# The last block's outputs finished bank by bank, with product P7 in two PSUM banks

## The chip, the cores and the metric

The kernel runs on one core of one Trainium2 chip. The metric is the device time of one execution in microseconds (us); a smaller number is better. A profile covers one such execution. Its span, from the first to the last instruction of the program, is a little shorter than the time of that execution.

## The reference, cut to what matters

A depthwise causal convolution with softmaxed taps (one set of 7 taps per head) is followed by two matrix products with a SiLU between them. All is fp32.

```python
w = softmax(weight, axis=-1)                       # (8 heads, 7 taps)
out[b, s, head, :] = sum_k w[head, k] * x_pad[b, s + k, head, :]
x = out.reshape(32768, 192)
h = x @ w_in                                       # (32768, 2048)
g = h * (1.0 / (1.0 + np.exp(-h)))                 # silu(h)
return g @ w_out                                   # (32768, 192)
```

## The kernel before, in words

The 32,768 tokens are worked in 32 blocks of 1,024, each of two token tiles of 512 (`TB`). The feature axis lies on the partitions, so a token tile is 512 columns of a PSUM bank. For each block VectorE computes the convolution, TensorE the products of `x @ w_in` (L442), ScalarE copies and applies SiLU (L457, L463), VectorE adds (L466), and TensorE then computes `g @ w_out` (L513). Work of the next block's convolution is interleaved into the present block by the strings of `PLAN`; `pin` keeps every engine's instructions in the order in which the program issues them.

From the second block on, both matrix products are done with seven instead of eight block products (Winograd's form of Strassen's algorithm). For `g @ w_out` the 2x2 split is: two token tiles against two halves of the 192 output channels, 96 (`HD`) each. The 2,048 hidden features are summed in four steps j = 0 to 3 (`NJ`), each with two sub-steps e. For each j VectorE first forms four combinations of silu(h) with `sum_g` (L483), named `t.j0` to `t.j3`: 128x1024 subtractions. They lie in tiles of the pool `tpool` (tag "t", three buffers), two combinations to a tile.

`out_slot(b, j, i, e)` issues the matmuls of one output bank i. A bank has 128 partitions and a product only 96 rows, so partitions 0 to 95 hold one product and partitions 96 to 127 a third of another: bank 0 is P1 with a third of P2, bank 1 is P3 with a third of P2, bank 2 is P6 with the last third of P2, bank 3 is P7 with a third of P4, bank 4 is P5 with a third of P4, and bank 5 holds the last third of P4 as four pieces of 128 columns. Each 32-row quarter is a matmul of its own; the profile shows two hardware matmuls for each. Banks 0 and 1 and P2 use silu(h) itself; bank 2 needs `t.j1`, bank 3 `t.j2` and `t.j3`, bank 4 `t.j0` and `t.j3`, bank 5 `t.j3`.

The outputs `c[0]` to `c[3]` (96 x 512 rows of the tile `cmb`, channel half i // 2 of token tile i % 2) are then sums of products: c0 = P1 + P2, c1 = P1 + P6 + P3 + P5, c2 = P1 + P6 + P7 + P4, c3 = P1 + P6 + P7 + P5. ScalarE copies the thirds of P2 into a tile `y` and those of P4 into a tile `x_`, so that they stand on the right partitions for VectorE. Each c[i] is transposed by VectorE into `osb` and stored by three DMAs, two issued from the queue of SP and one from that of ScalarE (L685).

In all blocks but the last these sums run beside the next block's matmuls. For the last block the program runs j = 0 and 1 through `down` with the plan's remaining slots (which include `t.20`), and then calls `finish` (L654), where the change lies. There TensorE's order before is: for j = 2, then j = 3, banks 2, 4, 3, 5; then bank 0 for both j; then bank 1 for both j, in two halves of 256 columns. VectorE forms each j's combinations ahead of that j's matmuls. The sums begin when banks 2 to 5 are full: c1 = P6 (L691), c2 and c3 with P7 and P5, P4 added to c2; then, when bank 0 is full, P1 to c3, c2 and c1, with c3 and c2 stored whole; ScalarE's copies of P1 and a third of P2 (L717, L718) follow. Last come, for each half, P3 to c1 (VectorE), the copy of the last third of P2 (L722), the store of c1, P2 to c0 (GpSimd, L724) and the store of c0. The adds, transposes and copies through `vec` and `act` are recorded under L111.

Of the kernel before, what the change touches and what calls it, by code (L numbers as in the profile page):

```python
# [9 lines left out]
F32 = mybir.dt.float32  # L10
I32 = mybir.dt.int32
AF = mybir.ActivationFunctionType
ALU = mybir.AluOpType
# [4 lines left out]
def kernel(  # L18
# [24 lines left out]
    nc = tc.nc  # L43
# [6 lines left out]
    P = 128  # L50
# [4 lines left out]
    TB = 512  # L55
    TT = 2 * TB
    NB = NT // TT
    NCH = DFF // P
    NM = NCH // 2
    NJ = NM // 2  # L60
    SQ = 32
    HD = D // 2
    NP = HD // SQ
# [6 lines left out]
    xpool = ctx.enter_context(tc.tile_pool(name="xp", bufs=1))  # L70
    tpool = ctx.enter_context(tc.tile_pool(name="tp", bufs=3))
# [31 lines left out]
    def pin(ins):  # L103
        return tc.keep_in_program_order(ins)
# [8 lines left out]
    vec, act = Pinned(nc.vector), Pinned(nc.scalar)  # L113

    def bank():
        return psum.tile([P, TB], F32, tag="ps", name="ps")
# [171 lines left out]
    for e in range(2):  # L288
        half = hot[R * e : R * e + R]
# [24 lines left out]
    for k in range(NK):  # L314
# [4 lines left out]
            op=ALU.mult,  # L319
# [98 lines left out]
    bk, us, sums, cmbs, accs = {}, {}, {}, {}, {}  # L418
# [32 lines left out]
    def sums_h(b, name, m):  # L451


        if name[0] == "s":
            u = us[b, m, name[1]] = upool.tile([P, TB], F32, tag="u", name="u")
            copy = nc.vector.tensor_copy if name == "s2" else nc.scalar.copy
            pin(copy(u, bk[b, m, "1"]))  # L457
            return
        g = g_of(b, m, int(name[1]) - 1, int(name[2]) - 1)
        if name == "C21":  # L460
            pin(nc.scalar.activation(g, bk[b, m, "1"], AF.Silu))
        elif name[0] == "g":
            pin(nc.scalar.activation(g, g, AF.Silu))  # L463
        else:
            i, bn = {"C11": ("1", "b"), "C22": ("3", "d"), "C12": ("2", "d")}[name]
            pin(nc.vector.tensor_tensor(g, us.pop((b, m, i)), bk[b, m, bn], op=ALU.add))  # L466
# [18 lines left out]
    def out_slot(b, j, i, e, half=None):  # L485

        g = [gs[b, j, a] for a in range(2)]
        w, x_ = wo[j], wx[j]  # L490
        if i not in accs.setdefault(b, {}):
            accs[b][i] = bank()

        def t(k):
            return sums[b, j][k // 2][:, k % 2, :].rearrange("p (e t) -> p e t", e=2)

        a_ = [[w[:, a, :, HD * u : HD * u + HD] for a in range(2)] for u in range(2)]
        forms = {
            1: lambda: (a_[0][0], g[0][:, 0]),
            2: lambda: (a_[0][1], g[1][:, 0]),  # L500
            3: lambda: (x_[:, 2], g[1][:, 1]),
            4: lambda: (a_[1][1], t(3)),
            5: lambda: (x_[:, 0], t(0)),
            6: lambda: (x_[:, 1], t(1)),
            7: lambda: (a_[1][0], t(2)),
        }
        own, other, c = ((1, 2, 0), (3, 2, 1), (6, 2, 2), (7, 4, 0), (5, 4, 1), (4, 4, 2))[i]
        for q in range(4):
            lhs, rhs = forms[own if q < NP else other]()
            k = c if i == 5 or q == NP else q  # L510
            to = slice(0, TB // 4) if i == 5 else slice(0, TB) if half is None else ts(half, TB // 2)
            pin(
                nc.tensor.matmul(  # L513
                    accs[b][i][SQ * q : SQ * q + SQ, to],
                    lhs[:, e, SQ * k : SQ * k + SQ],
                    rhs[:, e, ts(q, TB // 4) if i == 5 else to],
                    start=j == 0 and e == 0,
                    stop=j == NJ - 1 and e == 1,
                    skip_group_check=True,
                )  # L520
            )

    def down(b, j):

        for i in (0, 1, 2, 4, 3, 5) if j < NJ - 1 else (0, 1, 2, 3, 5, 4):
            for e in range(2):
                out_slot(b, j, i, e)
                yield
        for a in range(2):
            del gs[b, j, a]  # L530
# [63 lines left out]
    osbs = {}  # L594
# [21 lines left out]
    def step(b, token):  # L616

        if token[0] == "-":
            b, token = b - 1, token[1:]
        name, arg = token.split(".") if "." in token else ("", "")  # L620
        if b < 0 or b >= NB or not name or (b, token) in did:
            return
        did.add((b, token))
        digits = [int(c) for c in arg]
        if name[0] in "PE":
            product(b, digits[0], name)
        elif name[0] in "sCg":
            if b:
                sums_h(b, name, digits[0])
        elif name == "t":  # L630
            sum_g(b, *digits)
        elif name[0] in "Mzyx":
            merge(b, name)
        elif name == "o":
            turn_out(b, *digits)
        elif b + 1 < NB:
            {"i": turn_in, "v": conv, "w": win}[name](b + 1, *digits)
            if name == "v" and digits[1] == K - 1 and (b, "down") in did:
                spread(b + 1, digits[0])
                if digits[0] == NK - 1 and b + 2 < NB:  # L640
                    load(b + 2)
# [12 lines left out]
    def finish(b):  # L654


        late = (NJ - 2, NJ - 1)
        for j in late:
            for k in (0, 1, 3, 2):
                step(b, f"t.{j}{k}")  # L660
            for i in (2, 4, 3, 5):
                for e in range(2):
                    out_slot(b, j, i, e)
        acc, n = accs[b], HD
        cmb = xpool.tile([P, 4, TB], F32, tag="cmb", name="cmb")
        cmbs[b] = [cmb]
        c = [cmb[0:n, i, :] for i in range(4)]
        y, x_ = (upool.tile([P, TB], F32, tag="u", name="u") for _ in range(2))

        def part(t, k):  # L670
            return t[SQ * k : SQ * k + SQ, :]

        def add(out_, u, v):
            vec.tensor_tensor(out_, u, v, op=ALU.add)

        def store(i, cols, rows_=slice(0, n)):

            if b not in osbs:
                osbs[b] = tpool.tile([P, 4, TB // SQ, SQ], F32, tag="t", name="osb")
            osb = osbs[b][:, i, :, :].rearrange("p k c -> p (k c)")  # L680
            vec.transpose(osb[rows_, cols], cmb[rows_, i, cols])
            ks = slice(cols.start // SQ, cols.stop // SQ)
            for q in range(rows_.start // SQ, rows_.stop // SQ):
                ch = HD * (i // 2) + SQ * q
                (nc.sync, nc.scalar, nc.sync)[q % 3].dma_start(  # L685
                    out=out_v[2 * b + i % 2][:, ks, ch : ch + SQ],
                    in_=osbs[b][SQ * q : SQ * q + SQ, i, ks, :],
                )

        every = slice(0, TB)  # L690
        pin(nc.scalar.copy(c[1], acc[2][0:n, :]))  # L691
        pin(nc.scalar.copy(part(y, 2), acc[2][n:P, :]))
        pin(nc.scalar.copy(part(x_, 1), acc[4][n:P, :]))
        add(c[2], c[1], acc[3][0:n, :])
        pin(nc.scalar.copy(part(x_, 0), acc[3][n:P, :]))
        add(c[3], c[2], acc[4][0:n, :])
        add(c[1], c[1], acc[4][0:n, :])
        for q in range(4):
            pin(
                nc.scalar.copy(  # L700
                    part(x_, 2)[:, ts(q, TB // 4)], acc[5][SQ * q : SQ * q + SQ, 0 : TB // 4]
                )
            )
        add(c[2], c[2], x_[0:n, :])
        for j in late:
            for e in range(2):
                out_slot(b, j, 0, e)
        for half in range(2):
            for j in late:
                for e in range(2):  # L710
                    out_slot(b, j, 1, e, half)
            if half == 0:
                for k in (3, 2):
                    add(c[k], c[k], acc[0][0:n, :])
                    store(k, every)
                add(c[1], c[1], acc[0][0:n, :])
                pin(nc.scalar.copy(c[0], acc[0][0:n, :]))  # L717
                pin(nc.scalar.copy(part(y, 0), acc[0][n:P, :]))  # L718
        for half in range(2):
            cols = slice(half * TB // 2, (half + 1) * TB // 2)  # L720
            add(c[1][:, cols], c[1][:, cols], acc[1][0:n, cols])
            pin(nc.scalar.copy(part(y, 1)[:, cols], acc[1][n:P, cols]))  # L722
            store(1, cols)
            nc.gpsimd.tensor_tensor(c[0][:, cols], c[0][:, cols], y[0:n, cols], op=ALU.add)  # L724
            store(0, cols)


    for k in range(NK):
# [41 lines left out]
    for b in range(1, NB):  # L770
# [9 lines left out]
        slots = (None for j in range(NJ // 2 if last else NJ) for _ in down(b, j))  # L780
        for s, _ in zip(plan[NU:], slots):
            run(b, [s])
        assert next(slots, 0) == 0
    finish(NB - 1)


# [28 lines left out]
```

## Time and profile before

| | |
|---|---|
| Time, median of 4 runs | 2420.8 us (2420.28 to 2420.85) |
| The profiled execution's own time | 2420.28 us |
| Its span | 2418.5 us |
| Mean granted TensorE clock | 0.998 |
| Busy: TensorE / VectorE / ScalarE / GpSimd | 2387.2 / 2073.9 / 991.0 / 69.7 us |
| Share of the chain that ended last: PE / DMA | 98% / 1% |
| Last block's L513 matmuls begin | 2373.5 us after the span's start |

A profile names engines PE (TensorE; PEld is its weight load), DVE (VectorE), ACT (ScalarE), POOL (GpSimd) and SP; a q behind the name is the engine's sequencer or DMA queue. The chain that ended last follows the work back from the last instruction, at each step to what released it. A row of the timeline has start, duration, engine, line, operation, output<-input, shapes and, in brackets, the idle time before it and what ended that. All but some 45 us of the span lie ahead of the stage that the change touches.

### The profile page before, as it was taken

The page shows a single profiled execution, that of the slowest core. Times are in us where ns is not written, and L with a number is a line of the kernel's source. Part 1 is how long each engine was busy: PE and PEld are TensorE (multiplying, and loading weights), DVE is VectorE, ACT ScalarE, POOL GpSimd, SP SyncE. Part 2 cuts the span into 40 slices and gives each one's busy share as a digit, 9 for nine tenths or more (in the row PEclk, how much of TensorE's full clock was granted, in tenths as well). Part 3 has the DMA queues.
Part 4 walks back from the last instruction along what each step waited for, and adds up shares of the span by engine and source line. Part 5 has one row for each costly group of instructions (what it writes and reads, how often), then busy time and mean ns, then how long its engine had stood idle before and what let it go on. Part 6 is the DMA issues. An engine that isn't in the chain of part 4 may idle for free.

```text
span 2418.5 us, 43131 instructions
## 1 busy us (share of the span) xinstructions
PE 2387.2 (99%) x17776; PEld 937.3 (39%) x17776; DVE 2073.9 (86%) x2821; ACT 991.0 (41%) x1857; POOL 69.7 (3%) x98
## 2 busy tenths in 40 slices
PE   6999999999999999999999999999999999999998
PEld 3334433334433344333343333443334433334433
DVE  8889888898888888888988889888889888898876
ACT  3234533345433345333454334543334533345432
POOL 3300000000000000000000000000000000000000
PEclk9999999999999999999999999999999999999999
DMA  8321222222222212222222222122222222222220
GB/s 157 75 44 39 38 44 53 44 44 38 36 53 51 42 32 43 46 53 40 40 40 40 53 47 46 33 36 53 53 41 40 36 45 53 43 43 39 36 40 14
DMA packets 454085, 111.65 MB, mean 46 GB/s; under 512 B 423936, under 2 KB 429056, under 8 KB 453888
## 3 DMA queue, kind: packets, MB, share of 16 engines
q1 hardware_dynamic: 450064, 106.89, 23.8%
q8 instruction: 139, 2.28, 0.4%
q0 software_dynamic: 480, 1.58, 0.3%
q10 hardware_dynamic: 3344, 0.42, 0.1%
q14 instruction: 58, 0.48, 0.1%
HBM read 31.49 MB, written 25.17 MB: 23 GB/s over the span
## 4 chain that ended last, share of the span: by engine, by line
PE 98%; DMA 1%; DVE 0%; ACT 0%; SPq 0%; issue 0%; POOLq 0%; POOL 0%; ACTq 0%
PE ps L442 49%; PE ps L513 46%; PE ps L541 2%; PE ps L406 1%; DMA dup<-nat 0%; SPq L127 0%; DMA tail<-xt 0%; DVE nat L356 0%; DMA wexp<-in_weight_dram 0%; DMA nat<-in_x_dram 0%; ACT g L111 0%; ACT two L111 0%; DVE cmb L111 0%; DVE osb L111 0%; DVE two L111 0%
## 5 line engine op out<-in xcount | busy, mean ns | idle before, releaser
L442 PE MATMUL ps<-dup,ws 64*128 64x512 f32 x2480 | 869.9, 589 | 0.0
L513 PE MATMUL ps<-g,wo 128*32 128x512 f32 x2984 | 662.2, 592 | 0.0
L466 DVE TENSOR_TENSOR g<-u,ps 128x512 f32<-128x512 f32 x744 | 486.1, 681 | 119.1 <-PE ps L442 89.8
L442 PE MATMUL ps<-win,wr 64*128 64x512 f32 x1488 | 567.7, 589 | 0.0
L513 PE MATMUL ps<-t,wo 128*32 128x512 f32 (+1 forms) x4464 | 500.7, 450 | 0.0
L463 ACT ACTIVATE g<-g 128x512 f32<-128x512 f32 x744 | 444.8, 631 | 97.3 <-DVE g L466 97.3
L442 PEld LDWEIGHTS ps<-dup,ws 64*128 64x128 f32 x2480 | 363.0, 187 | 292.0 <-issue 277.9
L513 PE MATMUL ps<-t,wx 128*32 128x512 f32 x2976 | 452.9, 592 | 0.0
L356 DVE SCALAR_TENSOR_TENSOR nat<-xt,taps,nat 128x512 f32<-128x512 f32 x576 | 432.2, 751 | 18.7 <-ACT nat L351 3.8
L442 PE MATMUL ps<-dup,wr 64*128 64x512 f32 x992 | 419.9, 596 | 0.0
L457 ACT COPY u<-ps 128x512 f32<-128x512 f32 x496 | 278.1, 589 | 228.7 <-PE ps L442 225.7
L580 ACT COPY cmb<-ps 96x512 f32<-96x512 f32 x30 | 17.5, 582 | 805.3 <-PE ps L513 805.3
L483 DVE TENSOR_TENSOR t<-g,t 128x1024 f32<-128x1024 f32 x248 | 303.5, 1224 | 18.7 <-PE ps L513 8.3
L483 DVE TENSOR_TENSOR t<-g 128x1024 f32<-128x1024 f32 x248 | 299.9, 1220 | 22.8 <-PE ps L513 22.8
L442 PEld LDWEIGHTS ps<-win,wr 64*128 64x128 f32 x1488 | 233.4, 187 | 175.6 <-issue 147.2
L513 PEld LDWEIGHTS ps<-t,wo 128*32 128x32 f32 x4464 | 178.3, 110 | 222.6 <-issue 204.6
L442 PE MATMUL ps<-win,ws 64*128 64x512 f32 x496 | 242.2, 589 | 0.0
L513 PE MATMUL ps<-g,wx 128*32 128x512 f32 (+1 forms) x1512 | 234.6, 585 | 0.0
L513 PEld LDWEIGHTS ps<-t,wx 128*32 128x32 f32 x2976 | 121.9, 110 | 277.6 <-issue 268.3
L592 DVE TENSOR_TENSOR cmb<-cmb,ps 96x512 f32<-96x512 f32 x150 | 102.3, 682 | 135.2 <-ACT u L577 133.1
L442 PEld LDWEIGHTS ps<-dup,wr 64*128 64x128 f32 x992 | 160.5, 187 | 128.2 <-issue 114.0
L513 PEld LDWEIGHTS ps<-g,wo 128*32 128x32 f32 x2984 | 169.4, 110 | 98.3 <-issue 98.3
(66 smaller groups left out, 1206.8 us busy)
## 6 DMA issues: line engine op xcount, KB each, us to landing
dup<-nat SPq DMA_DIRECT2D x384, 128.0 KB, 2.3
nat<-in_x_dram SPq DMA_DIRECT2D x382, 64.0 KB, 2.4
out_dram<-osb SPq DMA_DIRECT2D x376, 64.0 KB, 2.0
raw<-in_moe_w_in_dram SPq DMA_DIRECT2D x16, 192.0 KB, 5.3
raw<-in_moe_w_out_dram SPq DMA_DIRECT2D x8, 384.0 KB, 3.9
ws<-wr POOLq DMA_DIRECT2D x8, 192.0 KB, 3.2
xt<-xt SPq DMA_DIRECT2D x31, 4.5 KB, 1.9
tail<-xt SPq DMA_DIRECT2D x24, 4.5 KB, 1.9
```

The source lines that it names most:

```text
L356: nc.vector.scalar_tensor_tensor(out=dst, in0=src, scalar=tap, in1=dst, op0=ALU.mult, op1=ALU.add)
L406: nc.tensor.matmul(hs[a, n, e], rows(wr[j], e)[:, a, k, :], rows(d, e)[:, n, k, :], start=k == 0, stop=k == NK - 1,)
L442: nc.tensor.matmul(bk[b, m, bn], rows(w, half), rows(v, half), start=first, stop=True, skip_group_check=True,)
L457: pin(copy(u, bk[b, m, "1"]))
L463: pin(nc.scalar.activation(g, g, AF.Silu))
L466: pin(nc.vector.tensor_tensor(g, us.pop((b, m, i)), bk[b, m, bn], op=ALU.add))
L483: pin(nc.vector.tensor_tensor(t[i // 2][:, i % 2, :], u, v, op=ALU.subtract))
L513: nc.tensor.matmul(accs[b][i][SQ * q : SQ * q + SQ, to], lhs[:, e, SQ * k : SQ * k + SQ], rhs[:, e, ts(q, TB // 4) if i == 5 else to], sta ...
L541: nc.tensor.matmul(acc[k][R * n : R * n + R, :], wo[j][:, a, e, R * k : R * k + R], gs[b, j, a][:, n, e, :], start=j == 0 and a == 0 and e ...
L580: pin(nc.scalar.copy(c[0], acc[0][0:n, :]))
L592: pin(nc.vector.tensor_tensor(out_, u, v, op=ALU.add))
```

## The change

In the last block P7 goes into two banks: its columns 0 to 255 into bank 3 and its columns 256 to 511 into a seventh bank, 6, for all four j (`down` and `out_slot`). In `finish` the order becomes bank by bank: the combinations `t.j0`, `t.j1` of both late j; bank 0 for both j, then bank 1; the combinations `t.j3`, `t.j2` of both j; then banks 2, 4, the first half of bank 3, bank 5, and the second half of P7 in bank 6. Each bank's sums follow it: ScalarE copies P1 and two thirds of P2 early; with bank 2 come c2 = P1 + P6, c1 with P3, c0 with P2 and the store of c0; with bank 4 come c1 and c3 with P5 and the store of c1; with each half of P7, c3 and c2, the store of c3's half, P4 to c2 and the store of c2's half. In each bank from bank 2 on VectorE's adds stand ahead of ScalarE's copy. GpSimd takes no part. The fourth tile of combinations and `osb` take the buffers of the tags "win" and "dup", which the last block's products no longer need.

The core of the diff:

```diff
-        if i not in accs.setdefault(b, {}):
-            accs[b][i] = bank()
+        at = 6 if i == 3 and half else i
+        if at not in accs.setdefault(b, {}):
+            accs[b][at] = bank()
...
-                    accs[b][i][SQ * q : SQ * q + SQ, to],
+                    accs[b][at][SQ * q : SQ * q + SQ, to],
...
             for e in range(2):
-                out_slot(b, j, i, e)
+                for half in range(2) if i == 3 and b == NB - 1 else (None,):
+                    out_slot(b, j, i, e, half)
                 yield
...
+        sums[b, NJ - 1] = {1: xpool.tile([P, 2, 2 * TB], F32, tag="win", name="t")}
...
-                osbs[b] = tpool.tile([P, 4, TB // SQ, SQ], F32, tag="t", name="osb")
+                osbs[b] = xpool.tile([P, 4, TB // SQ, SQ], F32, tag="dup", name="osb")
...
+        for j in late:
+            for k in (0, 1):
+                step(b, f"t.{j}{k}")
+        acc = accs[b]
+        slots(0)
+        act.copy(c[0], acc[0][0:n, :])
+        act.copy(part(y, 0), acc[0][n:P, :])
+        slots(1)
+        act.copy(part(y, 1), acc[1][n:P, :])
+        for k in (3, 2):
+            for j in late:
+                step(b, f"t.{j}{k}")
+        slots(2)
+        add(c[2], c[0], acc[2][0:n, :])
+        act.copy(part(y, 2), acc[2][n:P, :])
+        add(c[1], c[2], acc[1][0:n, :])
+        add(c[0], c[0], y[0:n, :])
+        store(0, every)
+        slots(4)
+        add(c[1], c[1], acc[4][0:n, :])
+        add(c[3], c[2], acc[4][0:n, :])
+        act.copy(part(x_, 1), acc[4][n:P, :])
+        store(1, every)
         for half in range(2):
             cols = slice(half * TB // 2, (half + 1) * TB // 2)
-            add(c[1][:, cols], c[1][:, cols], acc[1][0:n, cols])
-            pin(nc.scalar.copy(part(y, 1)[:, cols], acc[1][n:P, cols]))
-            store(1, cols)
-            nc.gpsimd.tensor_tensor(c[0][:, cols], c[0][:, cols], y[0:n, cols], op=ALU.add)
-            store(0, cols)
+            slots(3, half)
+            p7 = acc[6 if half else 3]
+            if half == 0:
+                slots(5)
+                for q in range(4):
+                    act.copy(
+                        part(x_, 2)[:, ts(q, TB // 4)], acc[5][SQ * q : SQ * q + SQ, 0 : TB // 4]
+                    )
+            add(c[3][:, cols], c[3][:, cols], p7[0:n, cols])
+            add(c[2][:, cols], c[2][:, cols], p7[0:n, cols])
+            act.copy(part(x_, 0)[:, cols], p7[n:P, cols])
+            store(3, cols)
+            add(c[2][:, cols], c[2][:, cols], x_[0:n, cols])
+            store(2, cols)
```

`slots(i, half)` is new and issues `out_slot(b, j, i, e, half)` for both late j and both e. The old order in `finish`, told above, is taken out.

More of the change, by code (lines that the diff above doesn't have):

```diff
@@ L657, in finish @@
         late = (NJ - 2, NJ - 1)
[L658 to L664, printed above, removed]
+        sums[b, NJ - 1] = {1: xpool.tile([P, 2, 2 * TB], F32, tag="win", name="t")}
         cmb = xpool.tile([P, 4, TB], F32, tag="cmb", name="cmb")
         cmbs[b] = [cmb]
+        n = HD
         c = [cmb[0:n, i, :] for i in range(4)]
         y, x_ = (upool.tile([P, TB], F32, tag="u", name="u") for _ in range(2))
+        every = slice(0, TB)
         def part(t, k):
@@ L674, in add, with store @@
             vec.tensor_tensor(out_, u, v, op=ALU.add)
-        def store(i, cols, rows_=slice(0, n)):
+        def store(i, cols):
             if b not in osbs:
-                osbs[b] = tpool.tile([P, 4, TB // SQ, SQ], F32, tag="t", name="osb")
+                osbs[b] = xpool.tile([P, 4, TB // SQ, SQ], F32, tag="dup", name="osb")
             osb = osbs[b][:, i, :, :].rearrange("p k c -> p (k c)")
-            vec.transpose(osb[rows_, cols], cmb[rows_, i, cols])
+            vec.transpose(osb[0:n, cols], cmb[0:n, i, cols])
             ks = slice(cols.start // SQ, cols.stop // SQ)
-            for q in range(rows_.start // SQ, rows_.stop // SQ):
+            for q in range(NP):
                 ch = HD * (i // 2) + SQ * q
-                (nc.sync, nc.scalar, nc.sync)[q % 3].dma_start(
+                (nc.sync, nc.scalar, nc.sync)[q].dma_start(
                     out=out_v[2 * b + i % 2][:, ks, ch : ch + SQ],
@@ L688, in store @@
                 )
[L690 to L708, printed above, removed]
+        def slots(i, half=None):
             for j in late:
                 for e in range(2):
[L711 to L718, printed above, removed]
+                    out_slot(b, j, i, e, half)
```

## Prediction

> **What bounds the kernel now.** The page comes first: who is busy, and whose work makes the chain that ended last.
>
> ```profile
> PE 2387.2 (99%) x17776; PEld 937.3 (39%) x17776; DVE 2073.9 (86%) x2821; ACT 991.0 (41%) x1857; POOL 69.7 (3%) x98
> PE 98%; DMA 1%; DVE 0%; ACT 0%; SPq 0%; issue 0%; POOLq 0%; POOL 0%; ACTq 0%
> ```
>
> TensorE is the bound, and the change takes no matmul work away. What it can move is the stretch in which TensorE has nothing left. So the second view is the chain in order of time, for the end of the run (start, length, what).
>
> ```profile
> 2373.51 32.83 PE ps L513 x352
> ...
> 2409.76 0.53 ACT cmb L717
> 2410.28 0.07 issue
> 2410.35 0.58 ACT u L718
> ...
> 2411.40 0.72 POOL cmb L724
> 2412.12 1.33 issue
> 2413.45 0.77 POOLq L810
> 2414.22 0.02 issue
> 2414.24 0.44 DVE osb L111
> ```
>
> Behind the matmuls the chain runs through ScalarE's copies of bank 0, two GpSimd adds and a last transpose, which ends at 2414.68. The stretches show how much there is to win (length; busy time of each engine).
>
> ```profile
> core 0: us, PE busy (x) PEld busy (x) DVE busy (x) ACT busy (x) POOL busy (x), PEclk, DMA share, GB/s
> 2406.10:2409.75 3.65, 3.64 (x68) 1.95 (x60) 3.24 (x5) 0.00 (x0) 0.00 (x0) 1.00 0.23 35
> 2409.75:2414.70 4.95, 0.00 (x0) 0.00 (x0) 2.48 (x6) 1.90 (x4) 1.44 (x2) 0.78 0.69 105
> 2414.70:2418.50 3.80, 0.00 (x0) 0.00 (x0) 0.00 (x0) 0.00 (x0) 0.00 (x0) 0.50 0.24 39
> ```
>
> TensorE works without a gap until 2409.75; 4.95 us of adds, copies and transposes follow, then 3.80 us of stores and closing semaphores. No edit of this stage can win more than about 8.7 us, 0.36%. Last, the timeline of ScalarE and of SP's queue, the groups by shape, and SP's waits:
>
> ```profile
> 2403.27 0.58 ACT L695 COPY u<-ps 32x512 f32<-32x512 f32 x1 [1.87 <-DVE cmb L111]
> 2409.76 0.58 ACT L717 COPY cmb<-ps 96x512 f32<-96x512 f32 x1 [4.83 <-DVE cmb L111]
> L111 DVE STREAM_TRANSPOSE osb<-cmb 96x256 f32<-96x256 f32 x4 | 1.8, 441 | 2.4 <-POOL cmb L724 2.3
> L111 DVE TENSOR_TENSOR cmb<-cmb,ps 96x256 f32<-96x256 f32 x2 | 0.8, 397 | 0.1
> L722 ACT COPY u<-ps 32x256 f32<-32x256 f32 x2 | 0.7, 367 | 1.7 <-DVE cmb L111 1.7
> SPq L685 <- DMA out_dram<-osb: 1.4, 3, 0.7
> 2415.70 0.32 SPq L685 DMA_DIRECT2D out_dram<-osb  x1
> ```
>
> Bank 0 was full at 2406.36 (VectorE's first add of it starts then), yet L717 ran only at 2409.76: VectorE read the bank three times first, with two transposes between, and ScalarE waited for the last read. That puts the copies of P1 and P2 into the tail. The last store was issued at 2415.70, 1.02 after the last transpose; SP had waited for earlier stores to land.
>
> **TensorE's end after the change.** A slot of 512 columns advances TensorE by 0.86 (bank 0, both j and e, four slots: 2402.67 to 2406.11, 3.43). A slot of 256 columns takes half: the four quarters of one pass start at 2406.32, 2406.54, 2406.75, a step of 0.215 against 0.43. So splitting P7, for j = 0 and 1 too, costs nothing by the rows; if each half slot had a fixed extra of 0.02 (the scatter of these steps), the 16 halves of P7 less the 8 of P3 in the old order would cost 0.16. The slots are the same set, so TensorE ends at 2409.74 again, if it never waits. Late slots begin at 2391.50, hence: bank 0 to 2394.93, bank 1 to 2398.36, bank 2 to 2401.79, bank 4 to 2405.22, P7's first half to 2406.94, bank 5 (four slots at a quarter width) to 2407.80, second half to 2409.51.
>
> Can TensorE wait? Bank 2 needs `t.21` and `t.31`. `t.21` ends at 2385.3 as now; `t.30`, in the buffer that j = 1's first tile leaves when its bank 4 is done (2389.34; the old `t.23` started at 2389.58 for that reason), runs 2389.58 to 2390.8 and `t.31` to 2391.9: 6.4 us ahead of 2398.36. `t.23`, `t.33`, `t.22`, `t.32` follow at 1.2 each, to 2396.7, ahead of bank 4 at 2401.79. The seventh bank takes one that the last products' sums have left: their VectorE adds and ScalarE activations end by 2375.7 and it is written first at about 2380.7. Cost nothing; if the cover failed, every us of lateness would be a us on the end.
>
> **The sums, step by step.** A bank is readable about 0.25 after its slots' end (bank 0: 2406.11, first add 2406.36). Durations: VectorE add 96x512 0.69, 96x256 0.40; transpose 0.71 and 0.44; ScalarE 512 wide 0.58, 256 wide 0.37, 128 wide 0.26; a store's issue on ScalarE's queue 0.38. The early copies (c0, y0, y1: 1.74 of ScalarE) leave the path: ScalarE idles from 2375.7 to 2399.05 now.
>
> Bank 2 is readable at 2402.05: c2 to 2402.74, c1 to 2403.40, c0 (its y2 copied 2402.76 to 2403.34) to 2404.09, transpose to 2404.80; c0 is stored 5 us before TensorE ends. Bank 4 at 2405.48: c1 to 2406.17, c3 to 2406.84, transpose of c1 to 2407.53. ScalarE copies x_1 to 2407.45 and issues its share of c1's store at 2407.56 (behind it: the copies of bank 5). First half of P7, readable at 2407.19: c3 2407.53 to 2407.93, c2 to 2408.31, transpose of c3 to 2408.75. Now a new wait: c2 needs x_, ScalarE has four copies of bank 5 first (2408.05 to 2409.10) and then x_0 (to 2409.47). VectorE idles 0.75, c2 runs 2409.50 to 2409.90, its transpose to 2410.36. The second half, readable at 2409.80, is behind that by 0.5: c3 to 2410.74, c2 to 2411.12, ScalarE's copy to 2411.52 beside c3's transpose (to 2411.56), c2 to 2411.96, transpose to 2412.42. Against 2414.68 that is 2.26 earlier: two GpSimd adds (1.44), their hops and ScalarE's two copies leave the tail, and three adds of VectorE with one copy come in.
>
> **The stores.** There are 18 DMAs before and after, the same sizes; two outputs are whole, two in halves. Keeping the lag between last transpose and last issue (1.02), the last issue is at 2413.44 and the span 2416.2. Bounds of the lag: 0.36 if no store waits (two SP issues of store c3 are 0.36 apart: 2407.81, 2408.17), which gives 0.7 more gain; and the waiting case below. The stores begin 3 us earlier and are spread over 8 us, not 7, so I take the lag as it is.
>
> Two pages of the Trainium skill bear on this. Of the lag to landing: a 32 KB store takes 1.6 us to land in the row (64 KB: 2.5), the very last one 1.82 (2415.70 to 2417.52). "DMA: Bandwidth & Descriptors", section on the two cost components, has a fixed 2.0 us per DMA, hardly dependent on size; by it, an estimate, the end would come 0.2 later and the halves would buy little, speaking against splitting c3 and c2. Of the order VectorE before ScalarE: the trace has ScalarE waiting 1.87 and 4.83 for VectorE's reads of other partitions of the same bank. "PSUM — Partial Sum Buffer", section on bank collisions, says that different 32-partition quadrants of one bank may be read at once, so that these waits are the program's and not the chip's; without them x_0's last copy could start 0.4 earlier, but VectorE is busy with the transpose until 2411.56, and the sum stays.
>
> **Numbers.** The profiled execution took 2420.28 for a span of 2418.5, the median of the runs is 2420.8, 0.5 above. The span loses 2.3: 2416.2; the median goes to 2418.5. A measurement of this kernel can tell some 0.2%, 4.84 us, from no change: by that bound 2.3 us is within.
>
> **The rivals.**
>
> The sums as above (chance 0.70): 2417.6 to 2419.3, from the lag's 0.7 to a lag 0.8 longer.
>
> ScalarE's queue holds the last copy (0.16). The second half's x_0 copy stands behind the issue of c2's first-half store. If that issue waits for the landing of an earlier store, as SP's did three times, and that store is ScalarE's own of c3, issued at 2410.5 because it in turn waited for c1's (2407.9 + 2.6), landing takes 1.7: 2412.2. The copy starts 1.5 late (2412.65 for 2411.15): 2420.0. For it: 1.4 us of such waits in the same queue set now. Against: ScalarE's issues show no wait of that kind now.
>
> Slower (0.08): the stores land in single file. If each of the last three waits for the one before, the second issue of c3's first half being at 2409.1, the last issue comes at 2409.1 + 3 landings + 1.4 (two steps of 0.36 and a last one of 0.66, as from 2415.04 to 2415.70): with 2.0 us each (the median of all stores on the page) 2416.5, 0.8 later than now, time 2421.6; with 2.6 2423.4. It decides above 1.74 us per landing. For it: the waits named. Against: only three of twelve SP issues waited, and 32 KB stores take 1.6.
>
> The change does nothing at the end (0.06): ScalarE's and VectorE's new order is not what the engines run, or TensorE ends later by what the tail wins: 2420.3 to 2421.
>
> For 0.2% either way it would take more than these: faster needs the lag and all 2.3 us of VectorE's chain behind TensorE gone, slower a stall of TensorE of 7 us, beyond both covers above. I give 0.02 and 0.04, and 0.94 between. The range leaves out the slower rival and the far end of a gain: 2417.4 to 2420.8.
>
> **What would show it.** Right: TensorE's last matmul still ends near 2409.74 without a gap from 2373.5; GpSimd absent; the last transpose near 2412.4 with VectorE idle about 0.75 for x_ in the first half; the last store issued near 2413.4. Wrong: a gap in L513 ahead of bank 2 or 4 (the combinations), ScalarE's last copy after 2412 behind a store's issue, or SP's waits on stores above 2 us.

## The result

The changed kernel takes 2418.3 us (median of 41 runs, 2417.86 to 2418.78) against 2420.8 us before: a ratio of 0.999, with a 95% interval of 0.9985 to 0.9994. It is 2.5 us faster, inside the prediction's bound of 0.2% (4.84 us), and 0.2 us from the forecast of 2418.5. The profiled execution of it has a span of 2416.4 us, 2.1 less than before.

The page of the changed kernel, its busy times and its chain:

```profile
PE 2387.8 (99%) x17808; PEld 940.3 (39%) x17808; DVE 2073.6 (86%) x2823; ACT 990.4 (41%) x1856; POOL 69.1 (3%) x96
PE 98%; DMA 1%; DVE 0%; ACT 0%; SPq 0%; issue 0%; ACTq 0%; DVEq 0%
```

TensorE has 32 more hardware matmuls (the halves of P7 for j = 0 and 1) and the same busy time to 0.6 us; GpSimd has lost its two adds and left the chain. The chain in order of time (start, length, what):

```profile
2373.78 34.58 PE ps L515 x416
...
2408.37 0.03 ACT u L111
...
2409.86 0.43 DVE cmb L111
...
2410.31 0.44 DVE osb L111
2410.76 0.65 DVE cmb L111 x2
...
2411.48 0.38 ACT u L111
...
2411.88 0.43 DVE cmb L111
...
2412.34 0.44 DVE osb L111
```

The chain now leaves TensorE already at 2408.35, for ScalarE's copies of bank 5, and goes through VectorE's add of P4 to c2, the first half's transpose, the second half's adds, its copy, its add and its transpose. (L515 is the old L513.) The stretches, with the columns as before (each begins 0.28 later than in the trace of before, as the stage itself did):

```profile
2406.38:2410.03 3.65, 3.65 (x84) 2.30 (x76) 2.46 (x7) 1.98 (x6) 0.00 (x0) 1.00 0.68 94
2410.03:2412.78 2.75, 0.00 (x1) 0.00 (x0) 2.54 (x7) 0.37 (x1) 0.00 (x0) 0.90 0.57 84
```

Between the end of the matmuls and the last transpose VectorE is busy 2.54 of 2.75 us, where before it was busy 2.48 of 4.95. ScalarE's copies (1.98 us for 0.00) and the stores (DMA share 0.68 for 0.23) have moved beside the matmuls.

Executions of one kernel differ by when the last stage begins: TensorE's first output matmul of the last block started at 2373.43 in the trace of before and at 2373.71 in that of after, and between 2373.3 and 2374.2 in the others; work up to there is the same in all. Medians can shift by some 0.5 us for that alone, so parts of the tail are compared below from this stage's start. "Last transpose" is the end of VectorE's last transpose counted from there, "lag" the time from that end to the last store's issue, "landing" from that issue to its landing. Some 0.9 to 1.0 us of closing semaphores follow in every run. Last transpose, lag and landing are of the one profiled execution of each run.

| Run | Time, us | Before, same group | Last transpose | Lag | Landing |
|---|---|---|---|---|---|
| before | 2420.8 | | 41.25 | 1.02 | 1.82 |
| after | 2418.3 | 2420.8 | 39.07 | 0.70 | 1.89 |
| u1_one_bank | 2419.2 | 2420.7 | 40.28 | 0.68 | 2.06 |
| u2_scalar_first | 2420.6 | 2420.7 | 41.49 | 0.91 | 1.84 |
| u3_gpsimd_add | 2418.7 | 2420.7 | 39.75 | 0.68 | 1.86 |
| u4_whole_p7 | 2418.85 | 2420.7 | 39.77 | 0.39 | 2.62 |
| u5_late_combos | 2423.9 | 2420.5 | 45.04 | 0.68 | 2.03 |
| b1_vector_add | 2420.2 | 2420.5 | 40.57 | 1.31 | 1.99 |
| b2_copies_early | 2421.7 | 2420.5 | 41.71 | 1.71 | 1.82 |
| n1_bank5_earlier | 2417.6 | 2420.5 | 38.82 | 0.68 | 1.87 |
| a2_changed_again | 2418.0 | 2420.9 | 39.07 | 0.70 | 2.24 |
| n2_queues | 2417.3 | 2420.9 | 39.07 | 0.39 | 1.69 |
| n3_both | 2417.5 | 2420.9 | 38.83 | 0.39 | 1.66 |

For the signs that the prediction named: SP's waits for landings in the changed kernel (before: 1.4 us in three waits), and ScalarE's last copy.

```profile
SPq L684 <- DMA out_dram<-osb: 0.4, 1, 0.4
2411.48 0.37 ACT L111 COPY u<-ps 32x256 f32<-32x256 f32 x1 [1.65 <-DVE cmb L111]
```

### The profile page after: what moved, and what is told of

It reads as the page before. It is cut to its first block, busy times and chain, and to the rows that moved or that the text cites. A ratio compares the mean times of both kernels' runs of the same rounds, so it can differ in the third digit from the quotient of the medians.

```text
span 2416.4 us, 43191 instructions
## 1 busy us (share of the span) xinstructions
PE 2387.8 (99%) x17808; PEld 940.3 (39%) x17808; DVE 2073.6 (86%) x2823; ACT 990.4 (41%) x1856; POOL 69.1 (3%) x96
## 4 chain that ended last, share of the span: by engine, by line
PE 98%; DMA 1%; DVE 0%; ACT 0%; SPq 0%; issue 0%; ACTq 0%; DVEq 0%
PE ps L442 49%; PE ps L515 46%; PE ps L544 2%; PE ps L406 1%; DMA nat<-in_x_dram 0%; DMA dup<-nat 0%; DMA tail<-xt 0%; DVE nat L356 0%; SPq L127 0%; ACT g L111 0%; ACT two L111 0%; DVE two L111 0%; DVE cmb L111 0%; ACT u L111 0%; ACT L111 0%
## 5 line engine op out<-in xcount | busy, mean ns | idle before, releaser
L515 PE MATMUL ps<-g,wo 128*32 128x512 f32 x2976 | 661.8, 593 | 0.0
L515 PE MATMUL ps<-t,wo 128*32 128x128 f32 (+2 forms) x4528 | 500.6, 446 | 0.0
L515 PE MATMUL ps<-t,wx 128*32 128x512 f32 x2976 | 452.7, 592 | 0.0
L515 PEld LDWEIGHTS ps<-t,wo 128*32 128x32 f32 x4528 | 180.3, 110 | 219.8 <-issue 199.5
L515 PE MATMUL ps<-g,wx 128*32 128x512 f32 x1488 | 234.6, 592 | 0.0
L515 PEld LDWEIGHTS ps<-t,wx 128*32 128x32 f32 x2976 | 121.9, 110 | 278.8 <-issue 269.6
L515 PEld LDWEIGHTS ps<-g,wo 128*32 128x32 f32 x2976 | 168.5, 110 | 98.3 <-issue 98.3
```

What stands on the lines that cost most here:

```text
L515: nc.tensor.matmul(accs[b][at][SQ * q : SQ * q + SQ, to], lhs[:, e, SQ * k : SQ * k + SQ], rhs[:, e, ts(q, TB // 4) if i == 5 else to], st ...
```

## Experiments: parts of the change undone

**P7 in one bank.**

```diff
-        at = 6 if i == 3 and half else i
+        at = i
...
-                for half in range(2) if i == 3 and b == NB - 1 else (None,):
-                    out_slot(b, j, i, e, half)
+                out_slot(b, j, i, e)
...
-            p7 = acc[6 if half else 3]
+            p7 = acc[3]
```

> The changed kernel with one part undone: P7 stays in one bank (3) for all four j and is only cut into two column halves for the last two j, as P3 was before the change. The theory (the end is set by the chain behind TensorE: each bank's reads and TensorE's writes to it exclude each other) expects TensorE to stop ahead of P7's second half until VectorE's two adds and ScalarE's copy of the first half are done (ScalarE's copy ended 36.05 us after the stage's start in the changed kernel), so that TensorE ends 1.7 us later than 36.2 and the last transpose comes about 1.1 us later than in the changed kernel; 2419.4 us. The rival (it is the order of the banks alone that brings the gain, the second bank is idle decoration) expects no difference from the changed kernel: 2418.3 us, and no gap in TensorE's matmuls.

Measured: 2419.2 us, the last transpose 1.21 later than in the changed kernel. The stretch in which TensorE stood still (columns as above), and from the timeline TensorE's matmuls and VectorE's adds of the second half:

```profile
2407.90:2409.60 1.70, 0.14 (x8) 0.03 (x5) 0.52 (x3) 1.39 (x5) 0.00 (x0) 1.00 0.70 97
```

```profile
2409.57 1.93 PE L515 MATMUL ps<-t,wo 128*32 128x256 f32 x32 [1.56 <-ACT u L111]
2411.57 0.75 DVE L111 TENSOR_TENSOR cmb<-cmb,ps 96x256 f32<-96x256 f32 x2 [1.12 <-PE ps L515]
```

TensorE is busy 0.14 of 1.70 us, because its writes to the bank wait for the reads of the first half, the last of which is ScalarE's copy. Its whole stage took 38.08 us for 36.33. In the changed kernel VectorE had no wait for TensorE at this point. The second bank is worth 1.2 us of the tail (0.9 in the medians).

**ScalarE ahead of VectorE in each bank.**

```diff
-        add(c[2], c[0], acc[2][0:n, :])
         act.copy(part(y, 2), acc[2][n:P, :])
+        add(c[2], c[0], acc[2][0:n, :])
...
+            act.copy(part(x_, 0)[:, cols], p7[n:P, cols])
             add(c[3][:, cols], c[3][:, cols], p7[0:n, cols])
             add(c[2][:, cols], c[2][:, cols], p7[0:n, cols])
-            act.copy(part(x_, 0)[:, cols], p7[n:P, cols])
```

(bank 4 in the same way)

> The changed kernel with ScalarE's copy put ahead of VectorE's adds in banks 2, 4, 3 and 6; nothing else. The theory (reads of one bank by the two engines exclude each other in this program, and ScalarE's queue holds four copies of bank 5 ahead of the first P7 copy) expects VectorE's first add of P7 to wait for a copy that can't end before 2409.8 (it started at 2407.60 in the changed kernel), and the last transpose about 1.8 us later: 2420.1 us. The rival (the two engines read different partitions, so the order doesn't matter and only the order of the banks counts) expects 2418.3 us with VectorE's add of P7 still at about 2407.6.

Measured: 2420.6 us, the last transpose 2.42 later. VectorE's two adds of P7, first and second half, and between them ScalarE's second copy:

```profile
2410.28 0.75 DVE L111 TENSOR_TENSOR cmb<-cmb,ps 96x256 f32<-96x256 f32 x2 [1.91 <-ACT u L111]
2412.56 0.37 ACT L111 COPY u<-ps 32x256 f32<-32x256 f32 x1 [2.31 <-DVE osb L111]
2412.96 0.75 DVE L111 TENSOR_TENSOR cmb<-cmb,ps 96x256 f32<-96x256 f32 x2 [0.79 <-ACT u L111]
```

Both halves wait for ScalarE. The second wait, 0.79, is what the expectation had too small: the second copy stood behind the issue of c2's first-half store on ScalarE's queue and began only at 2412.56, after that half's transpose (to 2412.16) and the issue. With this one part undone the last transpose (41.49) is no earlier than in the kernel before (41.25): the new order of the banks pays only together with the order of the reads.

**The last add on GpSimd.**

```diff
-            add(c[2][:, cols], c[2][:, cols], x_[0:n, cols])
+            nc.gpsimd.tensor_tensor(c[2][:, cols], c[2][:, cols], x_[0:n, cols], op=ALU.add)
```

> The changed kernel with the add of P4 to c2 (two halves) given back to GpSimd, as c0's add was before the change. The theory expects each of the two adds, both on the chain, to cost 0.72 for 0.42 and one more hop of some 0.05 to 0.1: the last transpose 0.7 to 0.8 us later, 2419.0 us. The rival (GpSimd leaving the end is the whole of the gain) expects 2420.8 us, that of the kernel before.

Measured: 2418.7 us, the last transpose 0.68 later. The two transposes of c2 wait for GpSimd:

```profile
2410.82 0.44 DVE L111 STREAM_TRANSPOSE osb<-cmb 96x256 f32<-96x256 f32 x1 [1.99 <-POOL cmb L732]
2413.18 0.44 DVE L111 STREAM_TRANSPOSE osb<-cmb 96x256 f32<-96x256 f32 x1 [0.93 <-POOL cmb L732]
```

The tail comes close to the expected 0.7 to 0.8. The medians, of different groups, show only 0.4, within the scatter of the stage's start. GpSimd's leaving is a part of the gain, not the whole.

**No halves.**

```diff
-        for half in range(2):
-            cols = slice(half * TB // 2, (half + 1) * TB // 2)
-            slots(3, half)
-            p7 = acc[6 if half else 3]
-            if half == 0:
-                slots(5)
+        for cols in (every,):
+            slots(5)
+            slots(3)
+            p7 = acc[3]
+            if True:
```

> The changed kernel without any halves: bank 5 ahead of bank 3, then P7 whole in bank 3, and c3 and c2 added, transposed and stored whole. The theory expects TensorE's end unchanged, behind it two adds of 0.68, a copy of 0.58 beside a transpose of 0.70, an add of 0.68 and a transpose of 0.70: the last transpose 0.7 us later than in the changed kernel, and the last stores of 64 KB to land 0.6 us slower (2.5 against 1.9): 2419.5 us. The rival (VectorE has so much queued that halving buys nothing) expects the last transpose where it is now and 2418.3 to 2418.9 us.

Measured: 2418.85 us, the last transpose 0.70 later, as expected. VectorE idles until the whole of P7 is there:

```profile
2409.67 1.28 DVE L111 TENSOR_TENSOR cmb<-cmb,ps 96x512 f32<-96x512 f32 x2 [2.40 <-PE ps L515]
```

The last store of 64 KB lands in 2.62 for 1.89, as expected, but its issue comes 0.39 after the last transpose for 0.70, with fewer stores ahead of it on SP's queue. The three terms together grew by 1.1, the median by 0.55; in the profiled execution the stage began 0.39 earlier than in that of the changed kernel, so the difference is within the scatter of that start.

**The combinations behind the first sums.**

```diff
-        for k in (3, 2):
-            for j in late:
-                step(b, f"t.{j}{k}")
         slots(2)
...
         store(0, every)
+        for k in (3, 2):
+            for j in late:
+                step(b, f"t.{j}{k}")
         slots(4)
```

> The changed kernel with t.j3 and t.j2 of both late j moved from ahead of bank 2 to behind the sums of bank 2 (behind the store of c0 and ahead of bank 4's matmuls). It measures the cover: the prediction had these four at no cost because they end 5 us ahead of their use, and every us of lateness beyond it a us on the end. The theory expects VectorE to begin t.23 at 2405.2, bank 4 to start at about 2406.5 instead of 2402.05, a stall of TensorE of 4.4 us, and all behind it as much later: 2422.7 us. The rival (the sums behind TensorE have slack that takes up part of it) expects 2 us or less over the changed kernel: up to 2420.3 us.

Measured: 2423.9 us (2422.39 to 2425.84, a far wider scatter than any other run's), the last transpose 5.97 later for the expected 4.4. TensorE's first matmul of bank 4 that needs `t.23` in the timeline, and two stretches:

```profile
2406.88 0.62 PE L515 MATMUL ps<-t,wo 128*32 128x512 f32 x1 [3.26 <-DVE t L483]
```

```profile
2403.40:2406.80 3.40, 0.22 (x3) 0.00 (x0) 3.26 (x6) 0.58 (x1) 0.00 (x0) 1.00 0.06 10
2406.80:2411.00 4.20, 4.12 (x24) 1.16 (x28) 3.43 (x4) 0.00 (x0) 0.00 (x0) 0.59 0.29 41
```

VectorE is busy 3.26 of 3.40 us while TensorE waits for `t.23`: no slack takes the stall up. The stall itself is near the expected 4.4: this matmul starts 32.68 us after the stage's start, and 28.40 after it in the changed kernel, so 4.3 later. (TensorE stood still for 3.26 of that; bank 4's matmuls of P5, which need only `t.20`, ran ahead of it.) The other 1.7 us are in the second stretch: the granted clock is 0.59 there. From 2407.4 to 2410.9 it was 0.5, and the passes of a slot stand 0.86 apart (they start at 2408.07, 2408.92 and 2409.78) instead of 0.43.

## Experiments: parts of the change alone, and one step further

**The kernel before, with the last add on VectorE.**

```diff
-            nc.gpsimd.tensor_tensor(c[0][:, cols], c[0][:, cols], y[0:n, cols], op=ALU.add)
+            add(c[0][:, cols], c[0][:, cols], y[0:n, cols])
```

> The kernel before with one part of the change alone: the add of P2 to c0 (two halves) on VectorE instead of GpSimd. The theory expects each of the two adds to take 0.42 for 0.72 plus hops, both on the chain: the last transpose 0.8 us earlier, 2420.0 us. The rival (GpSimd's two adds and hops are the whole gain) expects 2418.3 us.

Measured: 2420.2 us for 2420.5 of before in the same group; the last transpose 0.68 earlier, as expected within 0.1, but the lag 0.29 longer. SP's waits in this run (1.4 before):

```profile
SPq L685 <- DMA out_dram<-osb: 1.6, 3, 0.7
```

The store queue gave part of the win back: c1's and c0's half stores stand closer together, and SP waits for earlier ones to land.

**The kernel before, with the copies of bank 0 ahead of VectorE's reads.**

```diff
             if half == 0:
+                pin(nc.scalar.copy(c[0], acc[0][0:n, :]))
+                pin(nc.scalar.copy(part(y, 0), acc[0][n:P, :]))
                 for k in (3, 2):
...
-                pin(nc.scalar.copy(c[0], acc[0][0:n, :]))
-                pin(nc.scalar.copy(part(y, 0), acc[0][n:P, :]))
```

> The kernel before with ScalarE's two copies of bank 0 (P1 and a third of P2) moved ahead of VectorE's three adds from that bank, so that they are not in the tail. If reads of one bank exclude each other, VectorE's adds start 1.2 us later (2407.55 for 2406.36) and take as long, while ScalarE's copy of the first half of P2's last third now waits for VectorE alone: 0.2 to 0.5 us slower than before, 2421.1 us; the copies can only leave the tail when bank 0 is full earlier, that is with the new order of the banks. The rival (these copies in the tail cost their 1.2 us, wherever bank 0 stands) expects 2419.6 us.

Measured: 2421.7 us, 1.2 slower than before; the last transpose 0.46 later, in the expected 0.2 to 0.5, and the lag 0.69 longer, which was not expected. VectorE's first add of bank 0, ScalarE's copy of the second half of P2's last third with the store's issue ahead of it, and SP's waits:

```profile
2407.54 0.69 DVE L111 TENSOR_TENSOR cmb<-cmb,ps 96x512 f32<-96x512 f32 x1 [1.95 <-ACT u L714]
2413.08 0.35 ACTq L685 DMA_DIRECT2D out_dram<-osb  x1
2413.47 0.37 ACT L722 COPY u<-ps 32x256 f32<-32x256 f32 x1 [1.69 <-DMA out_dram<-osb]
```

```profile
SPq L685 <- DMA out_dram<-osb: 2.2, 2, 1.8
```

The copies do not leave the path by changing places with VectorE's reads; they push them by 1.2. And here one of the prediction's two store rivals is seen at work: SP waits for landings, 1.8 us once and 0.4 ahead of its last issue, which makes the lag longer. The other is not, though the profile puts the wait of ScalarE's copy, 1.69, down to a landing: the copy starts 0.04 after the end of ScalarE's issue of c0's first-half store (2413.08 to 2413.43), and that issue starts when c0's transpose ends (2413.05). In the kernel before the same copy stands behind the same issue (2412.63 to 2413.01, copy at 2413.04). So nothing of it waited for a landing.

**The changed kernel, with bank 5 ahead of P7.**

```diff
+        slots(5)
         for half in range(2):
...
             if half == 0:
-                slots(5)
                 for q in range(4):
```

> The changed kernel with bank 5's matmuls between bank 4 and P7's first half, not between P7's halves; ScalarE's copies of bank 5 and all sums keep their order. It tests that VectorE's wait for x_ in the first half (1.20 us in the changed kernel) sits on the chain. The theory expects ScalarE's copies of bank 5 to begin right behind x_1's (2407.75 for 2408.37), P7's first half to be readable at 2408.3, the wait to go and c2's add to come at 2409.45 for 2409.86: the last transpose 0.4 us earlier, 2417.9 us. The rival (VectorE's own work from P7's second bank on sets the end, and the wait is cover) expects 2418.3 us.

Measured: 2417.6 us (2420.5 before in its group; the changed kernel beside another group has 2418.0 for 2420.9, so the times alone don't settle it), the last transpose 0.25 earlier for the expected 0.4. VectorE's wait for x_ in the first half, in the changed kernel and in this one:

```profile
2409.86 0.42 DVE L111 TENSOR_TENSOR cmb<-cmb,u 96x256 f32<-96x256 f32 x1 [1.20 <-ACT u L111]
```

```profile
2408.04 0.75 DVE L111 TENSOR_TENSOR cmb<-cmb,ps 96x256 f32<-96x256 f32 x2 [0.70 <-PE ps L515]
...
2409.28 0.42 DVE L111 TENSOR_TENSOR cmb<-cmb,u 96x256 f32<-96x256 f32 x1
```

The wait of 1.20 is gone; 0.70 of it has become a wait for TensorE ahead of P7's first half, which is now readable later. The wait was on the chain, and most of what was to be had from it went to that new one. The profile puts ScalarE's last copy of this run (2410.90) down to a store's landing; but it starts 0.09 behind the end of VectorE's adds of that half (2410.10 and 0.71), just as in the changed kernel (2410.68 and 0.71, copy at 2411.48), so no time went there.

**The base once more, the queues of c3's second half exchanged, and both.**

```diff
-        def store(i, cols):
+        def store(i, cols, queues=(nc.sync, nc.scalar, nc.sync)):
...
-                (nc.sync, nc.scalar, nc.sync)[q].dma_start(
+                queues[q].dma_start(
...
-            store(3, cols)
+            store(3, cols, (nc.scalar, nc.sync, nc.scalar) if half else (nc.sync, nc.scalar, nc.sync))
```

> The changed kernel itself, as the base on the same chip for the two runs beside it. Theory and rivals alike: 2418.3 us.

> The changed kernel with the three DMAs of c3's second half issued ScalarE, SP, ScalarE and not SP, ScalarE, SP, so that SP has one issue less ahead of the last store. In the changed kernel the last store's second SP issue came 0.67 after the first, where SP's two issues of a store without others close before it were 0.36 apart. If SP's queue is still working on the issues ahead, the last issue comes 0.3 us earlier: 2418.0 us. The rival (the transfers themselves limit the end, whichever queue issues them) expects the last landing and the time unchanged: 2418.3 us.

> The changed kernel with both: bank 5 ahead of P7's first half, and the queues of c3's second half exchanged. The theory expects the two to add, the first having measured 2417.6 us in another group of runs: 2417.3 us. The rival (with VectorE's chain shorter the stores stand closer together and land later) expects 2417.6 us or more.

Measured: 2418.0, 2417.3 and 2417.5 us. In the two with exchanged queues the lag is 0.39 for 0.70, the expected 0.3, and the last store lands in 1.66 to 1.69 us for 1.89 to 2.24. SP's two issues of the last store, in the changed kernel and with exchanged queues:

```profile
2412.80 0.32 SPq L684 DMA_DIRECT2D out_dram<-osb  x1
2413.47 0.32 SPq L684 DMA_DIRECT2D out_dram<-osb  x1
```

```profile
2412.97 0.32 SPq L684 DMA_DIRECT2D out_dram<-osb  x1
2413.33 0.45 SPq L684 DMA_DIRECT2D out_dram<-osb  x1
```

They stand 0.67 and 0.36 apart. So it was SP's queue that held the last issue; what in it needs the time is not shown. Both together have the shortest tail: last transpose, lag and landing add to 40.88 us, against 41.15 with the queues alone and 42.01 in the run of the changed kernel beside them. That they add is seen in the tail (the last transpose of one, 38.83, and the lag of the other, 0.39) and not in the medians (2417.5 and 2417.3): the eleven times of the run with both fall into two groups, 2416.97 to 2417.05 and 2417.51 to 2417.58, and the median happens to lie in the upper one. Lowest against lowest the three are 2417.76, 2417.22 and 2416.97. Both versions beat both kernels; which of the two is better the times don't settle.

## Why the prediction was right, step by step

- **TensorE's end.** Halving P7 was costed at nothing, 0.16 at most. The stage's matmuls took 36.33 us for 36.31, and no matmul of it waited. Right. (The steps of 0.215 that the prediction reads are between passes of four quarters, two to a slot, not between the quarters of one pass; its sum is the same.)
- **The covers.** No gap came ahead of bank 2 or 4; `t.32` ended at 2396.96 for 2396.7. The late combinations showed what stands behind this zero: the stall of 4.3 us beyond the cover went to the end in full, as the prediction had it, and, which it did not have, another 1.7 us with it.
- **The sums.** The forecast of the last transpose, 2412.42, is 38.99 after the stage's start in before; measured were 39.07. The single row that was off is VectorE's wait for x_: 1.20, not 0.75. VectorE reached it earlier (two adds 96x256 in 0.71, not 0.78; bank 4's two in 1.28, not 1.36; each transpose begins some 0.07 before the adds ahead of it end), and the add behind the wait came within 0.08 of the forecast (2409.86 less the 0.28 by which the stage began later, for 2409.50). So the larger wait cost nothing against the sum.
- **The stores.** "I take the lag as it is", 1.02, was mis-sized: 0.70. Before, SP's first issue of the last store came 0.36 after the transpose, held by a landing; in the changed kernel it came after 0.02. The second issue came 0.66 and 0.67 behind the first, as the prediction read it. The last landing was slower by 0.07 (0.42 in a second execution). So the tail is shorter by 2.43 us (2.18, and 0.32, less 0.07), where the sum had 2.26. The sum held because the tail that it added up was the right one; that its time came within 0.2 us is in part luck, as the lag was not in it and the times scatter by some 0.5 us with the stage's start.
- **Where the 2.5 us came from.** Of the last transpose's 2.18, undoing the order of reads alone takes back 2.42, the second bank 1.21, the halves 0.70 and GpSimd's add 0.68. These don't add: together they are more than twice the whole. The order of the banks was not undone by itself. Moving ScalarE's copies alone loses time, and VectorE's add alone wins 0.68 in the tail and 0.3 in the time.
- **The rivals.** ScalarE's last copy started when VectorE's reads were done, at 2411.48, and not behind a store; SP's stores did not land in single file. SP held by landings was seen in the kernel with early copies (1.8 us at the longest), so that chance was not idle. ScalarE's queue held by a landing was seen in no run; in the kernel with ScalarE ahead the last copy did stand behind a store's issue, but one that waited for its transpose.
- **The skill's pages.** "PSUM — Partial Sum Buffer" (bank collisions) allows two engines to read different 32-partition quadrants of one bank at once. No run here shows this: in all of them the program made the second reader wait, and the kernel that differs in their order alone lost 2.42 us of its tail to that. "DMA: Bandwidth & Descriptors" (the two cost components) has a fixed 2.0 us, nearly whatever the size, fitted to DMAs of the software path. The stores here, issued from SP and ScalarE, landed otherwise: in 1.66 to 2.24 us for the last ones of 32 KB, 2.62 for that of 64 KB. The measurement decides, and halving the last stores did buy something: 0.73 in the landing, of which the longer lag took back 0.31.

## What to carry to other kernels

The gain of an end stage is found by following the chain behind the bound engine and asking of each piece whether its input could be ready earlier: put first the banks whose sums are long, last the one with the shortest work behind it, and give a bank that is read in halves a second bank, so that the writes of the second half need not wait for the reads of the first. Where two engines read one bank in turn, the order of the two can be worth the whole change; the one that the chain needs reads first. Here a queue of stores held the end as an engine does: which queue issued the stores ahead of the last one was worth 0.31 us, nearly as much as an add of 0.42.

## What the hardware showed that was not expected

After TensorE had stood still for some 3.3 us in the kernel with late combinations, its granted clock was 0.5 for 3.41 us, 0.6 us after it had begun again, and its passes took 0.86 for 0.43; this cost 1.7 us on top of the stall. A stand of 1.5 us (P7 in one bank, 2408.05 to 2409.57 on its chain) did not lower the clock. "TensorE: Matmul & The Clock Gate" of the Trainium skill (section "What's actually happening") speaks of a free-running activity window of 4096 cycles, some 3.4 us; the length of the slow stretch agrees. The lowest of this kernel's ten times, 2422.39, is 4.1 above the changed kernel's median, about the stall alone. That the ten times of this kernel scatter over 3.4 us, twice the 1.7 us that one slow stretch cost, while the others scatter within 1 us, fits a window whose phase differs from run to run, but only one execution was profiled, and it is not shown.
